# VectorE's sum of the third output bank in tiles 2 to 4 put behind the third token chunk's normalisation, and batch 6's key turn behind the third product

## The chip, the cores and the metric

One NeuronCore of a Trainium2 chip runs the whole kernel; the other cores are idle. The metric is the device time of one execution in microseconds, as the median of several runs. The engines are TensorE (PE, matrix products; PEld is its weight load), VectorE (DVE), ScalarE (ACT), GpSimd (POOL) and SyncE (SP, which issues DMAs). Each has its own queue of instructions and works through it in order; semaphores hold an instruction until what it needs is there.

## The reference

Attention over keys and values that are pooled by eight, and behind it a feed-forward layer whose hidden units are the largest of three products:

```python
k_p = k.reshape(B, H, Sp, 8, D).mean(axis=3)      # B, H, S, D = 8, 8, 576, 64; Sp = 72
v_p = v.reshape(B, H, Sp, 8, D).mean(axis=3)
scores = q @ k_p.transpose(0, 1, 3, 2) / sqrt(D)
attn = softmax(scores)
x = (attn @ v_p).transpose(0, 2, 1, 3).reshape(B * S, H * D)     # 4608 tokens x 512
h = maximum(maximum(x @ w1, x @ w2), x @ w3)                     # 768 hidden units
out = h @ w_out                                                  # 4608 x 512
```

## The kernel before

**Two streams on one PE queue.** The attention goes batch by batch (eight of 576 tokens), the feed-forward layer by tiles of 512 tokens (nine, numbered 0 to 8). While PE works on tile n, the attention of batch n+1 is put between its products by hand. The kernel schedules nothing by itself: each engine's queue has its instructions in the order in which the Python code records them. For tiles 1 to 4 this order stands in the strings of `MIDDLE` (line 886), which `middle` (line 909) reads step by step; tile 5's first half is `block(5, LEAD, ...)` (line 939), and the rest follows another string, `ORDER`.

**The steps of a string.** `h` is the next product of the hidden layer (line 364, in tiles `pw`, ScalarE's relu on line 370, VectorE's maximum on line 372). `s0` to `s7` are the scores of one head (line 220, then exp on ScalarE). `v0` to `v4` are the five token chunks of a batch: `values` multiplies weights by values into a PSUM tile `pav` (line 270), VectorE takes the reciprocal `rcp` of the sums (line 276) and multiplies it in, which gives `xn` (line 278; this is the chunk's normalisation). `x0` to `x4` turn `xn` into `xT` with a transposing DMA on SP's queue (line 255). `T` turns a batch's queries with such a DMA (line 304). `k` is the key turn: `keys` transposes the pooled keys `kp` on PE into the PSUM tile `pkt` (line 201), and `turn_k` copies it into the two key tensors `kz` (line 210), first two copies on VectorE, then two on ScalarE; the second pair waits for the first. Tokens such as `k7<` and `v6+2` load and fold inputs on GpSimd's queue.

**The output of tiles 2 to 4 by seven products.** With w1 folded into w_out, a tile's output is one product over 1280 columns (`xT` and `hT`), and it is taken as a 2 by 2 block product with seven products in place of eight. `outs(i, 0, 1)` in `middle` issues product `i` for both 128-token rows `m` (ten matmuls, line 718); product 2 comes as two halves, `2l` and `2h` (five matmuls each). Products 1, 6, 5 and 3 add up in one PSUM bank `oA`, 7 and 4 in `oC`, and 2 has `oB`. What becomes of a product stands in `evict` (line 722):

```python
if i in (1, 5, 6, 3):
    copy(int(i in (5, 3)), lo if i in (1, 3) else hi)     # ScalarE, line 728
elif i == 2:
    plus(0, lo, "B")                                      # VectorE, line 731
elif i == 4:
    plus(0, hi, "C")
if i in (5, 7) and (12 - i, m) in done:
    plus(1, hi, "C")
```

So after product 5 ScalarE copies `oA` into the result tile `osb`, and VectorE adds the third bank `oC` to it as soon as that copy is done. In the string of tiles 2 and 3, chunk `v3` follows product 5, then come `2h`, `v4`, 3 and 4. In tile 4 chunks `v3` and `v4` follow product 5, then come `2h`, batch 6's key turn `6:k`, 3 and 4.

**What is shared.** PSUM tiles come from small rings: `att` (two tiles) serves the scores, the `pav` of each chunk and `pkt`; `pw` (three tiles) serves the hidden products and the banks `oB` and `oC`; `tr` (one tile) serves `oA`. A tile is written again only when its last reader is done. So `pkt` in tile 4 waits for `xn` of chunk `v3`, product 4 waits for the reader of `oC`, and the second and third hidden products of the next tile wait for the readers of `oB` and `oC`. Right after tile 4, block 5 issues one hidden product, then the first scores of batch 6 (which read both `kz` tensors), then the second hidden product.

Of the kernel before, what the change touches and what calls it, by code (L numbers as in the profile page):

```python
# [14 lines left out]
def kernel(  # L15
# [46 lines left out]
    def psum(shape, dtype, name, tag, bufs):  # L62
        return pools[-1].tile(shape, dtype, name=name, tag=tag, bufs=bufs)
# [86 lines left out]
    def tokens(t0, t1, k0=0, k1=KCH):  # L150

        t0, t1 = t0 % RING, (t1 - 1) % RING + 1
        assert t0 < t1
        return xT[:, k0:k1, t0:t1]
# [244 lines left out]
    def new_two():  # L399
        return sb3.tile([128, 2, C], F32, name="osb", tag="osb", bufs=3)  # L400
# [127 lines left out]
    PA, BC, PO = ("pa", 2), ("bc", 1), ("po", 1)  # L528
# [32 lines left out]
    def turns(n):  # L561
        return (pad3 if n % 2 else pad)[:, 0:4]
# [17 lines left out]
    def out_w(z, r0, r1):  # L580

        i, j = divmod(z, 2)
        c = slice(HALF * i, HALF * i + HALF)
        return (wm_sb[:, 2 * j + r0:2 * j + r1, c] if r1 <= 2
                else wo_sb[:, JH * j + r0 - 2:JH * j + r1 - 2, c])

    def out_s(z):
        return so_new[0][:, z - 1]
# [56 lines left out]
    def out_seven(n):  # L645

        mid = len(pools) < 3
        if mid:
            o = {}
        else:  # L650
            o = sb2.tile([128, 2304], F32, name="ob", tag="et")[:, 0:2048].rearrange(
                "p (j m c) -> p j m c", j=2, m=2)
            o = [o[:, 0], o[:, 1]]
        lo, hi = slice(0, HALF), slice(HALF, C)
        banks, done = {}, set()

        def store(e, j, c):
            for u in range(2):
                b, g = divmod(2 * (4 * n + 2 * j) + u, NG)
                pair = g + 2 < NG and GS[g + 2] == GS[g] + 4  # L660
                for m in range(0, 2, 1 + pair):
                    b, g = divmod(2 * (4 * n + 2 * j + m) + u, NG)
                    dst = out[S * b:S * b + S, :].rearrange("(r g) c -> r g c", g=NG)
                    e.dma_start(out=dst[:, GS[g]:GS[g] + 4 * pair + 1:4, c],
                                in_=o[j][64 * u:64 * u + 64, m:m + 1 + pair, c])

        def bank(of, m):
            if n < LAST:
                if of not in banks:
                    if mid:  # L670
                        tag = TR if of == "A" else PW
                        banks[of] = psum([128, 2, HALF], F32, name=f"o{of}", tag=tag[0],
                                         bufs=tag[1])
                    elif of == "A":
                        banks["A"] = psum([128, 2, 2, HALF], F32, name="oA", tag="val",
                                          bufs=1)[:, 0]
                    else:
                        tag = (PO, SC)[of == "C"]
                        banks[of] = psum([128, 2, HALF], F32, name=f"o{of}", tag=tag[0],
                                         bufs=tag[1])  # L680
                return banks[of]
            if (of, m) not in banks:
                tag = {"A": PA, "B": SC, "C": BC if m == 0 else SC}[of]
                banks[of, m] = psum([128, 2, HALF], F32, name=f"o{of}", tag=tag[0],
                                    bufs=tag[1])[:, 0:1]
            return banks[of, m]

        def product(i, *ms):
            if mid:
                for r in range(5):  # L690
                    for m in ms:
                        matmuls(i, m, (r,))
            else:
                for m in ms:
                    matmuls(i, m)
            done.update((i, m) for m in ms)
            if not mid:
                evict(i, ms)
            elif (i, 1) in done:
                evict(i, (0, 1))  # L700

        def matmuls(i, m, rows=range(5)):
            of = "B" if i == 2 else "C" if i in (4, 7) else "A"
            p = bank(of, m)[:, m if n < LAST else 0]
            za, zb = PRODUCTS[i]
            for r in rows:
                c = slice(128 * m, 128 * m + 128)
                if isinstance(zb, str):
                    z = int(zb[1]) - 1
                    left = (tt_all[0][:, z, r, c] if mid else  # L710
                            turns(n)[:, z, r, c] if r < 2 else th[n][z][:, r - 2, c])
                else:
                    at = HALF * (zb % 2) + 128 * m
                    left = (tokens(NB * n + at, NB * n + at + 128)[:, 2 * (zb // 2) + r] if r < 2
                            else hTs[n][:, JH * (zb // 2) + r - 2, at:at + 128])
                right = (out_s(int(za[1]))[:, r] if isinstance(za, str)
                         else out_w(za, r, r + 1)[:, 0])
                nc.tensor.matmul(  # L718
                    p, left, right, stop=(r == 4), skip_group_check=True,
                    start=(i in FIRST and r == 0 and (m == 0 or n == LAST)))  # L720

        def evict(i, ms):
            m, at = ms[0], slice(ms[0], ms[-1] + 1)

            def copy(j, c):
                if j not in range(len(o)):
                    o[j] = new_two()
                nc.scalar.copy(out=o[j][:, at, c], in_=bank("A", m))  # L728

            def plus(j, c, of):  # L730
                nc.vector.tensor_tensor(out=o[j][:, at, c], in0=o[j][:, at, c],
                                        in1=bank(of, m), op=ALU.add)

            def ended(*parts):
                return all((z, k) in done for z in parts for k in range(2))

            if i in (1, 5, 6, 3):
                copy(int(i in (5, 3)), lo if i in (1, 3) else hi)
            elif i == 2:
                plus(0, lo, "B")  # L740
            elif i == 4:
                plus(0, hi, "C")
            if i in (5, 7) and (12 - i, m) in done:
                plus(1, hi, "C")
            if n == LAST and i in (5, 7) and ended(5, 7):
                store(nc.sync, 1, hi)
            if n == LAST and i == 3 and ended(3):
                store(nc.scalar, 1, lo)
            if n < LAST and i in (5, 7, 3) and ended(5, 7, 3):
                store(nc.sync, 1, slice(0, C))  # L750
            if n == LAST and i in (2, 4) and ended(i):
                store((nc.gpsimd, nc.sync)[i // 4], 0, (lo, hi)[i // 4])
            if n < LAST and i in (2, 4) and ended(2, 4):
                store(nc.sync, 0, slice(0, C))

        return product
# [102 lines left out]
    def weave():  # L859

        products, seen = {}, {}
        for name in ORDER.split():
# [29 lines left out]
        2: """  # L892
            h k k5< q5< v5< h a1 a3 a2 a4 S S ! v3+2 h h s0 h s1 h s2 h s3 h s4 b1 f f ! k4+1 h s5
            h s6 h s7 h b2 b3 b4 ! k4+2 v4+1
            1 v0 x0 2l v1 x1 6 7 v2 x2 5:T 5 v3 x3 2h v4 x4 3 4
        """,
        3: """
            h k k6< q6< v6< h a1 a3 a2 a4 f ! v4+2 h h s0 h s1 h s2 h s3 h s4 b1 f ! k5+1 h s5
            h s6 h s7 h b2 b3 b4 ! k5+2 v5+1
            1 v0 x0 2l v1 x1 6:T 6 7 v2 x2 5 v3 x3 2h v4 x4 3 4  # L900
        """,
        4: """
            h k k7< q7< v7< h a1 a3 a2 a4 f ! v5+2 h h s0 h s1 h s2 h s3 h s4 b1 f ! k6+1 h s5
            h s6 h s7 h b2 b3 b4 f ! k6+2 v6+1
            1 v0 x0 v1 x1 2l 7:T 6 7 v2 x2 5 v3 x3 v4 x4 2h 6:k 3 4 v6+2 k7+3 v7+3
        """}
    folds = iter([f for wi in range(1, 3) for f in [fold_w(wi)] * 4])

    def middle(n):

        pieces, outs, out_tiles = hidden(n), None, project(n)
        for name in MIDDLE[n].split():
            if name == "h":
                next(pieces)
            elif name == "F":
                next(out_tiles)
            elif name == "f":
                next(next(folds))
            elif name == "!":
                held[:] = gate  # L920
            elif name.isdigit():
                outs = outs or out_seven(n)
                outs(int(name), 0, 1)
            elif name in ("2l", "2h"):
                outs = outs or out_seven(n)
                outs(2, "lh".index(name[1]))
            elif name[0] in "ab":
                sums_of(n, name)
            elif name[2:3] in ("<", "+"):
                pool_step(n, name)  # L930
            else:
                b, _, step = name.rpartition(":")
                do(int(b or n + 1), step)
        assert next(pieces, None) is None

    tt_all.append(const.tile([128, 4, 5, HALF], F16, name="tt", tag="tt"))
    for n in range(1, 5):
        middle(n)
# [12 lines left out]
    outs = out_seven(LAST)  # L951
# [36 lines left out]
```

## Time and profile before

| what | value |
| --- | --- |
| runs | 226.40, 226.49, 227.48 us; median 226.49 us |
| profiled execution | 226.51 us, of which 224.8 us are the span of the profile |
| PE busy | 215.1 us (96% of the span) |
| DVE, ACT, POOL busy | 149.4, 122.0, 139.8 us |
| tile 2's output products | about 90 to 99 us from the span's start |
| tile 3's | about 111 to 120 us |
| tile 4's | about 133 to 143 us |

Times are counted from the start of the span. A row of the timeline has the start, the length, the engine, the line, the operation with its tensors (out, arrow, in), the shape and how many instructions stand in the row; in brackets stands the engine's idle time before it and what ended it. Rows of PE overlap, since the next matmul begins before the last has drained.

### The profile page before, as it was taken

The page shows a single profiled execution, that of the slowest core. Times are in us where ns is not written, and L with a number is a line of the kernel's source. Part 1 is how long each engine was busy: PE and PEld are TensorE (multiplying, and loading weights), DVE is VectorE, ACT ScalarE, POOL GpSimd, SP SyncE. Part 2 cuts the span into 40 slices and gives each one's busy share as a digit, 9 for nine tenths or more (in the row PEclk, how much of TensorE's full clock was granted, in tenths as well). Part 3 has the DMA queues.
Part 4 walks back from the last instruction along what each step waited for, and adds up shares of the span by engine and source line. Part 5 has one row for each costly group of instructions (what it writes and reads, how often), then busy time and mean ns, then how long its engine had stood idle before and what let it go on. Part 6 is the DMA issues. An engine that isn't in the chain of part 4 may idle for free.

```text
span 224.8 us, 4685 instructions
## 1 busy us (share of the span) xinstructions
PE 215.1 (96%) x1806; PEld 146.6 (65%) x1807; DVE 149.4 (66%) x292; ACT 122.0 (54%) x221; POOL 139.8 (62%) x111
## 2 busy tenths in 40 slices
PE   7788999999999999999999998899999999999993
PEld 2477745557655545875596567555677777788882
DVE  4668877037594395786579668636667886898840
ACT  2277524755875478238733862484786446554330
POOL 7974400999949967787768757999600903772020
PEclk9999999999999999999999999999999999999999
DMA  6999999989749999749999998963341533200266
GB/s 175 209 197 197 204 207 205 206 152 231 143 105 163 235 201 226 127 105 160 242 206 175 167 263 115 172 172 57 71 103 28 123 63 86 47 3 0 62 199 163
DMA packets 50710, 33.54 MB, mean 149 GB/s; under 512 B 27040, under 2 KB 46368, under 8 KB 50688
## 3 DMA queue, kind: packets, MB, share of 16 engines
q0 software_dynamic: 20304, 16.98, 48.1%
q1 hardware_dynamic: 29936, 15.87, 31.8%
q10 hardware_dynamic: 448, 0.39, 0.7%
q8 instruction: 14, 0.23, 0.4%
q14 instruction: 8, 0.07, 0.1%
HBM read 34.60 MB, written 9.44 MB: 196 GB/s over the span
## 4 chain that ended last, share of the span: by engine, by line
PE 71%; DMA 12%; POOL 11%; issue 2%; DVE 1%; ACT 1%; POOLq 0%
PE pw L364 21%; PE oA L718 10%; DMA vt<-in_v_dram 8%; PE pA L794 7%; PE po L418 7%; PE oC L718 5%; PE po L414 5%; PE psc L220 4%; DMA mw<-in_moe_w_dram 4%; PE pC L794 3%; PE pav L270 3%; POOL half L163 3%; PE oB L718 2%; POOL half L164 2%; PE pB L794 2%
## 5 line engine op out<-in xcount | busy, mean ns | idle before, releaser
L364 PE MATMUL pw<-xT,mw 128*128 128x512 f16 (+1 forms) x336 | 72.8, 349 | 0.3 <-ACT xT L264 0.2
L364 PEld LDWEIGHTS <-mw 128*128 128x128 f16 x336 | 31.6, 98 | 20.4 <-issue 0.6
L372 DVE TENSOR_TENSOR hT<-t,pw 128x512 f16<-128x512 f16 (+1 forms) x42 | 25.4, 608 | 23.8 <-ACT et L225 16.4
L225 ACT ACTIVATE et<-psc 72x576 f16<-72x576 f32 (+2 forms) x54 | 35.1, 660 | 6.4 <-PE psc L220 6.3
L163 POOL TENSOR_TENSOR half<-vt 72x2048 f32<-72x2048 f16 x7 | 28.4, 4061 | 13.8 <-DMA vt<-in_v_dram 13.3
L164 POOL TENSOR_TENSOR half<-half 72x1024 f32<-72x1024 f32 (+1 forms) x13 | 27.3, 2098 | 10.7 <-DVE rcp L276 6.1
L370 ACT ACTIVATE t<-pw 128x512 f16<-128x512 f32 (+1 forms) x42 | 22.5, 537 | 14.7 <-PE pw L364 14.3
L278 DVE TENSOR_TENSOR xn<-pav,rcp 128x512 f16<-128x512 f32 x40 | 27.6, 691 | 1.4
L220 PE MATMUL psc<-qT,kz 128*128 128x320 bf16 (+2 forms) x120 | 22.6, 278 | 1.1 <-DVE qT L196 0.9
L418 PE MATMUL po<-mwo,hT 128*128 128x512 f16 (+1 forms) x102 | 23.5, 367 | 0.0
L220 PEld LDWEIGHTS <-kz 128*128 128x128 bf16 x143 | 13.1, 98 | 13.6 <-ACT qT L196 1.1
L163 POOL TENSOR_TENSOR half<-ktFalse 96x1536 f32<-96x1536 f16 x6 | 18.8, 3131 | 4.0 <-issue 2.9
L800 ACT CAST pad<-pA 128x512 f16<-128x512 f32 x27 | 15.5, 587 | 7.2 <-PE pA L794 7.0
L566 POOL TENSOR_TENSOR pad<-xT 128x256 f16<-128x256 f16 x8 | 5.9, 734 | 21.7 <-ACT pad L800 12.9
L270 PEld LDWEIGHTS <-et 72*128 72x128 f16 x320 | 15.3, 98 | 3.6 <-issue 0.4
L276 DVE RECIPROCAL rcp<-pav 128x8 f32<-128x8 f32 x40 | 8.1, 202 | 14.1 <-PE pav L270 13.9
L270 PE MATMUL pav<-vp,et 72*128 72x65 f16 x320 | 16.6, 194 | 0.1
L414 PE MATMUL po<-wm,xT 128*128 128x512 f16 (+1 forms) x68 | 16.6, 366 | 0.0
L728 ACT COPY osb<-oA 128x512 f32<-128x512 f32 x12 | 7.0, 585 | 16.7 <-PE oA L718 16.7
L423 ACT COPY osb<-po 128x512 f32<-128x512 f32 (+1 forms) x16 | 9.2, 573 | 12.0 <-PE po L418 11.3
L774 DVE SCALAR_TENSOR_TENSOR hT<-pad 128x512 f16<-128x512 f16 x18 | 14.1, 797 | 2.3 <-ACT pad L804 1.9
L794 PEld LDWEIGHTS <-sw 128*128 128x128 f16 x144 | 13.6, 98 | 2.5
(122 smaller groups left out, 382.4 us busy)
## 6 DMA issues: line engine op xcount, KB each, us to landing
out_dram<-osb SPq DMA_DIRECT2D x38, 128.0 KB, 5.2
ktFalse<-in_k_dram POOLq DMA_DIRECT2D x7, 576.0 KB, 8.3
qb<-in_q_dram POOLq DMA_DIRECT2D x7, 576.0 KB, 12.0
vt<-in_v_dram POOLq DMA_DIRECT2D x7, 576.0 KB, 16.7
mw<-in_moe_w_dram POOLq DMA_DIRECT2D x9, 256.0 KB, 9.3
out_dram<-osb SPq DMA_DIRECT2D x8, 256.0 KB, 5.6
ktTrue<-in_k_dram SPq DMA_DIRECT2D x3, 384.0 KB, 5.1
out_dram<-ob SPq DMA_DIRECT2D x8, 128.0 KB, 2.5
```

The source lines that it names most:

```text
L163: yield e.tensor_tensor(out=f, in0=t[:, :, 0:4, :], in1=t[:, :, 4:8, :], op=ALU.add)
L164: yield e.tensor_tensor(out=f[:, :, 0:2, :], in0=f[:, :, 0:2, :], in1=f[:, :, 2:4, :], op=ALU.add)
L220: nc.tensor.matmul(out, kz_all[b % 2][f % 2][rows, h, :], qTs[b][rows, n + i0:n + i1, 64 * (h % 2):64 * (h % 2) + 64], start=True, stop=True)
L225: nc.scalar.activation(out=out, in_=in_, func=FT.Exp, scale=1.0 / 64.0)
L270: nc.tensor.matmul(pav[:, h // 4, 65 * (h % 4):65 * (h % 4) + 65], ets[b][:, h, c0:c0 + 128], vp_all[:, b, h, :], start=True, stop=True)
L278: nc.vector.tensor_tensor(out=xn, in0=pv[:, :, :, 0:D], in1=rcp.to_broadcast([128, 2, 4, D]), op=ALU.mult)
L364: mm = nc.tensor.matmul(pw, w_sb[wi][:, kc, bass.ts(jc, 128)], x[:, kc], start=(kc == 0), stop=(kc == KCH - 1))
L372: nc.vector.tensor_tensor(out=hT[:, jc, c0:c1], in0=t, in1=pw, op=ALU.max)
L414: nc.tensor.matmul(po, tokens(128 * m, 128 * m + 128)[:, kc], wm_sb[:, kc, c], start=(kc == 0), stop=False)
L418: nc.tensor.matmul(po, hT[:, jc, bass.ts(mm, 128)], wo_sb[:, jc, c], start=False, stop=(jc == JCH - 1))
L718: nc.tensor.matmul(p, left, right, stop=(r == 4), skip_group_check=True, start=(i in FIRST and r == 0 and (m == 0 or n == LAST)))
L794: mm = nc.tensor.matmul(p[:, w], a[:, kc, bass.ts(g, 128)], b[:, kc, :], start=(i in FIRST and w + kc == 0), stop=(w + kc == 2), skip_grou ...
```

## The change

In tiles 2 to 4 product 5's copy on ScalarE stays where it was. VectorE's sum of `oC` after it becomes a step of its own, `e5`, recorded behind chunk `v3`'s normalisation. VectorE's sum of `oB` becomes a step `e2`, recorded behind `v4`. In tiles 2 and 3 chunk `v4` also moves ahead of `2h`, and in tile 4 `2l` moves ahead of `v1`. In tile 4 the key turn `6:k` moves from ahead of product 3 to behind it, and `e2` comes behind the key turn. No instruction is added or dropped. The order on SP's and GpSimd's queues stays the same. On ScalarE's queue only the two key copies and the copy of product 3 change places in tile 4.

```diff
@@ product
+            if not ms:
+                evict(i, (0, 1), True)
+                return
             if mid:
...
             if not mid:
                 evict(i, ms)
-            elif (i, 1) in done:
+            elif i != 2:
                 evict(i, (0, 1))
@@ evict
-        def evict(i, ms):
+        def evict(i, ms, summed=False):
...
-            if i in (1, 5, 6, 3):
+            if summed:
+                plus(i == 5, (lo, hi)[i == 5], "BC"[i == 5])
+            elif i in (1, 5, 6, 3):
                 copy(int(i in (5, 3)), lo if i in (1, 3) else hi)
...
-            if i in (5, 7) and (12 - i, m) in done:
+            if not mid and i in (5, 7) and (12 - i, m) in done:
                 plus(1, hi, "C")
@@ MIDDLE, tile 2
-            1 v0 x0 2l v1 x1 6 7 v2 x2 5:T 5 v3 x3 2h v4 x4 3 4
+            1 v0 x0 2l v1 x1 6 7 v2 x2 5:T 5 v3 x3 e5 v4 x4 2h e2 3 4
@@ MIDDLE, tile 3
-            1 v0 x0 2l v1 x1 6:T 6 7 v2 x2 5 v3 x3 2h v4 x4 3 4
+            1 v0 x0 2l v1 x1 6:T 6 7 v2 x2 5 v3 x3 e5 v4 x4 2h e2 3 4
@@ MIDDLE, tile 4
-            1 v0 x0 v1 x1 2l 7:T 6 7 v2 x2 5 v3 x3 v4 x4 2h 6:k 3 4 v6+2 k7+3 v7+3
+            1 v0 x0 2l v1 x1 7:T 6 7 v2 x2 5 v3 x3 e5 v4 x4 2h 3 6:k e2 4 v6+2 k7+3 v7+3
@@ middle
+            elif name in ("e2", "e5"):
+                outs(int(name[1]))
```

## The prediction

> **What bounds the kernel now.** I read the page first: the span, the busy times and the engines' shares of the chain that ended last.
>
> ```profile
> span 224.8 us, 4685 instructions
> PE 215.1 (96%) x1806; PEld 146.6 (65%) x1807; DVE 149.4 (66%) x292; ACT 122.0 (54%) x221; POOL 139.8 (62%) x111
> PE 71%; DMA 12%; POOL 11%; issue 2%; DVE 1%; ACT 1%; POOLq 0%
> ```
>
> PE is busy for 96% of the span and carries most of the chain, so an edit of VectorE's order is worth only what it takes from PE's idle time. I therefore asked for PE's busy time in the three stretches that the edit touches (the output products of tiles 2, 3 and 4).
>
> ```profile
> 88.30:99.00 10.70, 10.70 (x120) 9.01 (x119) 7.60 (x17) 4.10 (x7) 9.05 (x4) 1.00 0.69 120
> 110.10:120.40 10.30, 10.30 (x118) 8.81 (x117) 7.15 (x17) 3.71 (x7) 7.92 (x4) 1.00 1.18 229
> 131.70:143.30 11.60, 10.34 (x121) 8.72 (x119) 8.93 (x19) 2.92 (x6) 8.95 (x5) 1.00 0.91 177
> ```
>
> After the stretch come its length and PE's busy time; the clock column reads 1.00. In tiles 2 and 3 PE is never idle: there is nothing to gain there, only something to lose. In tile 4 it is idle for 11.60 - 10.34 = 1.26 us. The waits from 138 to 145 us say why.
>
> ```profile
> PE pkt L201 <- DVE rcp L276: 1.3, 1, 1.3
> DVE osb L731 <- ACT osb L728: 0.8, 1, 0.8
> PEld L220 <- ACT kz L210: 0.5, 1, 0.5
> ```
>
> One wait of 1.3 us at the key turn, and a smaller one at the next scores, behind ScalarE's copies of the keys. The timeline has the whole story.
>
> ```profile
> 137.21 0.43 PE L270 MATMUL pav<-vp,et 72*128 72x65 f16 x8
> 137.68 0.21 DVE L276 RECIPROCAL rcp<-pav 128x8 f32<-128x8 f32 x1 [0.17 <-PE pav L270]
> 137.92 0.69 DVE L278 TENSOR_TENSOR xn<-pav,rcp 128x512 f16<-128x512 f32 x1
> ...
> 138.57 0.69 PE L270 MATMUL pav<-vp,et 72*128 72x65 f16 x16
> 138.77 0.58 ACT L728 COPY osb<-oA 128x512 f32<-128x512 f32 x1 [1.86 <-PE oA L718]
> ...
> 139.31 0.49 PE L718 MATMUL oB<-mwo,hT 128*128 128x256 f16 x3
> 139.38 0.69 DVE L731 TENSOR_TENSOR osb<-osb,oC 128x512 f32<-128x512 f32 x1 [0.78 <-ACT osb L728]
> 139.99 0.20 DVE L276 RECIPROCAL rcp<-pav 128x8 f32<-128x8 f32 x1
> 140.22 0.69 DVE L278 TENSOR_TENSOR xn<-pav,rcp 128x512 f16<-128x512 f32 x1
> ...
> 140.83 0.20 DVE L276 RECIPROCAL rcp<-pav 128x8 f32<-128x8 f32 x1
> ...
> 141.06 0.29 PE L201 MATMUL pkt<-ident,kp 96*128 96x96 bf16 x3 [1.26 <-DVE rcp L276]
> ...
> 141.19 0.60 PE L718 MATMUL oA<-so,xT 128*128 128x256 f16 x4
> ...
> 141.67 0.68 DVE L731 TENSOR_TENSOR osb<-osb,oB 128x512 f32<-128x512 f32 x1
> ...
> 142.27 0.97 DVE L210 COPY kz<-pkt 64x288 bf16<-64x288 bf16 x2
> 142.28 0.60 PE L718 MATMUL oC<-wm,tt 128*128 128x256 f16 x4
> ...
> 143.37 1.03 PE L364 MATMUL pw<-xT,mw 128*128 128x512 f16 x4
> 143.57 0.69 DVE L731 TENSOR_TENSOR osb<-osb,oC 128x512 f32<-128x512 f32 x1 [0.34 <-PE oC L718]
> 143.60 0.97 ACT L210 COPY kz<-pkt 64x288 bf16<-64x288 bf16 x2 [4.25 <-PE oC L718]
> ...
> 144.75 1.03 PE L364 MATMUL pw<-xT,mw 128*128 128x512 f16 x4
> ```
>
> The matmuls of chunks v3 and v4 start at 138.57. VectorE could normalise v3 at once, but ahead of that its queue holds the sum of the third bank, which waits until ScalarE's copy of product 5 ends (138.77 + 0.58 = 139.35). So v3's reciprocal comes at 139.99 and its xn ends at 140.22 + 0.69 = 140.91. The key turn needs the PSUM tile that this xn reads, and goes at 141.06; products 3 and 4, which need none of this, stand behind it on PE's queue.
>
> **The change, part by part.** Tile 4 first, worked out with the rows above.
>
> VectorE. From a chunk's first matmul to its reciprocal the row of v2 has 137.68 - 137.21 = 0.47, so v3's reciprocal goes at 138.57 + 0.47 = 139.04. From reciprocal to xn it is 0.24 (137.68 to 137.92), from xn or a sum to the next instruction 0.61 (140.22 to 140.83; 139.38 to 139.99). Hence v3's xn 139.28 to 139.97, the sum e5 from 139.89 to 140.58 (ScalarE's copy ended at 139.35, so it no longer waits), v4's reciprocal 140.50, its xn 140.74, the two key copies at 140.74 + 0.61 = 141.35 if pkt is there, ending at 141.35 + 0.97 = 142.32 in place of 143.24. Then the sums of the second and third bank, about 142.3 to 143.0 and 142.9 to 143.6. Two things bring the copies forward: 139.38 - 139.04 = 0.34 of waiting at the head, and 0.60 of the second bank's sum, which now stands behind them.
>
> PE. The half product 2h issues its last three matmuls from 139.31; at 1.09 / 10 = 0.109 each (ten of product 3 from 141.19 to 142.28) the next can go at 139.64. Product 3 takes its place there, until 140.73; it accumulates on oA, whose reader ended at 139.35. The key turn then finds its tile free (xn ended at 139.97) and takes 141.19 - 141.06 = 0.13; product 4 goes at 140.86, after e5's end at 140.58, and the next tile's first hidden product at 141.95 in place of 143.37: 1.42 earlier. That the key turn's cover is good is seen from pkt: done by 140.73 + 0.29 = 141.02, ahead of the copies at 141.35.
>
> What is late next: ScalarE's key copies, which the next scores need. They follow VectorE's.
>
> ```profile
> 121.61 0.97 DVE L210 COPY kz<-pkt 64x288 bf16<-64x288 bf16 x2
> ...
> 122.67 0.96 ACT L210 COPY kz<-pkt 64x288 bf16<-64x288 bf16 x2 [0.59 <-DVE kz L210]
> ```
>
> Here they start 122.67 - 122.58 = 0.09 after VectorE's end; in tile 4 it was 143.60 - 143.24 = 0.36, for which no row gives a reason. With 0.09 they run from 142.41 to 143.38. The second hidden product started 144.75 - 144.57 = 0.18 after their end, so it now starts at 143.56: 1.19 earlier. With 0.36 it would be 143.83, 0.92 earlier. I take 0.09, which is what an identical pair showed in tile 3. So of the 1.42 that PE wins, 0.23 are given back in a longer wait at the first scores. ScalarE's copy of product 3, now ahead of its key copies, ends by about 141.6 and delays nothing.
>
> The other waits of the next tile: the second hidden product needs the reader of oB (about 143.0, against 143.56), the third the reader of oC (about 143.6, against 143.56 + 1.1 = 144.7). Both are covered, by 0.5 and 1.1. The move of 2l ahead of v1 costs nothing: VectorE takes v1 behind v0 either way. GpSimd and SP keep their order.
>
> Does the rest follow? One resource keeps its own time, GpSimd's fold of batch 7.
>
> ```profile
> 151.90 1.00 POOL L166 TENSOR_TENSOR kp<-half 96x384 bf16<-96x384 f32 x1
> ...
> 156.48 0.29 PE L201 MATMUL pkt<-ident,kp 96*128 96x96 bf16 x3
> ```
>
> Its keys are ready at 152.90 and used at 156.48, or 155.3 then: 2.4 of slack. Everything else behind tile 4 hangs on PE, so I let the 1.19 reach the end.
>
> The first hidden product also needs chunk x1 of batch 5 in xT.
>
> ```profile
> L255 SPq DMA_TRANSPOSE xT<-xn x2: 1208/1848/2487, 136.7 to 138.0; - x2
> DMA to landing us min/median/max: 3.7/4.0/4.3
> ```
>
> These are x0 and x1, issued at 136.7 and 138.0; the second landed 3.7 or 4.3 later, between 141.7 and 142.3, so at 141.95 it may be just there or 0.35 short. At the later end the first product waits, but the scores behind it still wait for ScalarE until 143.38, so the price is nothing at either end. The Trainium skill (Perfetto Trace Analysis, section "DMA Instruction — HWDGE (DVE, Sync)") says that the bar of such an instruction covers the making of descriptors and not the movement of data: by the bar (138.0 + 2.49 = 140.5) there would be 1.4 us to spare. The trace agrees with the page: the landing row is 1.2 us or more behind the bar, and the sum by it stays the same only because ScalarE is later still.
>
> Tiles 2 and 3. PE's order changes only between chunk v4 and 2h. The one new risk is product 4, which now waits for e5 behind v3.
>
> ```profile
> 95.76 0.42 PE L270 MATMUL pav<-vp,et 72*128 72x65 f16 x8
> ...
> 97.92 0.60 PE L718 MATMUL oC<-wm,tt 128*128 128x256 f16 x4
> ```
>
> With the same steps, v3's reciprocal goes at 95.76 + 0.47 = 96.23, xn at 96.47, e5 from 97.08 to 97.77. Product 4 follows at 97.92, and PE reacted to xn in tile 4 after 141.06 - 140.91 = 0.15. So it just fits: 0 to 0.1 lost per tile, nothing gained since PE is never idle there; I take 0. The sums of oB and oC end about where they did.
>
> **Sum.** 226.51 (profiled execution; span 224.8 plus 1.7 around it) - 1.19 = 225.3 us. The median of the runs shown, 226.49, is the same within 0.02. That is 0.53% less. About 0.5%, or 1.13 us, is what a measurement of this kernel can tell from no change.
>
> **Rivals.**
> 1. *ScalarE's copies take back more.* If the 0.36 of tile 4 is their habit in this place, the gain is 0.92, and with 0.1 lost in each of tiles 2 and 3 it is 0.7: 225.6 to 225.8, within 0.5%. For it speaks that the 0.36 stood in this tile; against it the 0.09 of tile 3.
> 2. *A transfer or a fold takes the place of the wait.* If x1 lands over 0.5 us later than in this run, or GpSimd's fold slips by over 2.4, the gain shrinks by each further 0.1: about 226.0 to 226.5. The transposing DMA of x1 took 2487 ns where the other took 1208, so it does vary; but a later landing than 4.3 is seen in neither.
> 3. *Slower: product 4 becomes the place.* If v3's normalisation in tiles 2 and 3 isn't early, because something else than the third bank's sum holds it, then e5 and the reader of oC are late, and PE stalls in stretches where it never did. Were v3's reciprocal to go 0.95 later, at 97.18, e5 would end at 98.72 and product 4 start at 98.87: 0.95 in each of two tiles, 1.9, less 1.19: 227.2. It decides from 0.15 us of lateness on and turns the sign at 0.75 in each tile. Against it speaks that VectorE sat idle for 0.8 ahead of that sum in tile 4, so nothing else was held up.
>
> **How the numbers follow.** The forecast has 0.62, rivals 1 and 2 together 0.31 (0.22 and 0.09), rival 3 has 0.07. The forecast's cases reach from 225.1 (PE keeps all of the 1.42) to 225.4; rivals 1 and 2 go to 226.5. I give 224.9 to 226.5: 0.2 below the first for the spread of the runs, and up to rival 2's end; rival 3 stays outside. Faster by over 0.5% is the forecast, 0.62; within 0.5% are rivals 1 and 2, 0.31; slower 0.07.
>
> **What would show it.** Right: the wait of the key turn for rcp is gone; PE's idle time from product 1 of tile 4 to the next tile's first hidden product falls from 1.26 to below 0.2; v3's reciprocal in tile 4 goes about 0.5 after its matmuls and e5 right behind its xn; the scores' wait for ScalarE's key copies grows from 0.5 to about 0.7. Wrong: an idle PE ahead of product 4 in tile 2 or 3, a gap ahead of the first hidden product of the next tile put down to xT, or a second hidden product that starts later than 143.9.

## The result and the profile after

| | before | after |
| --- | --- | --- |
| median of 22 runs each | 226.49 us | 225.93 us (225.21 to 226.25) |
| ratio after / before | | 0.9976, 95% interval 0.9967 to 0.9985 |
| profiled execution; span | 226.51; 224.8 us | 225.68; 224.0 us |

The changed kernel is faster by 0.24%, which is 0.54 us with an interval of 0.34 to 0.75. The forecast was 1.19 us. By the bound of 0.5% this lies within no change, the case to which the prediction gave 0.31.

The page of after, in the same order as before's: span, busy times, engines' shares of the chain that ended last.

```profile
span 224.0 us, 4682 instructions
PE 214.2 (96%) x1806; PEld 146.6 (65%) x1807; DVE 149.4 (67%) x292; ACT 122.4 (55%) x221; POOL 140.1 (63%) x111
PE 86%; DVE 5%; DMA 3%; ACT 2%; issue 1%; SPq 0%; DVEq 0%; ACTq 0%
```

PE is still the bound. The three stretches of output products (stretch, its length, PE's busy time first):

```profile
88.30:99.00 10.70, 10.70 (x120) 9.01 (x119) 7.96 (x17) 3.92 (x7) 9.05 (x4) 1.00 0.68 117
110.10:120.40 10.30, 10.30 (x119) 8.81 (x117) 7.59 (x16) 3.52 (x7) 7.92 (x4) 1.00 1.20 241
131.70:143.30 11.60, 11.32 (x126) 9.26 (x124) 9.52 (x20) 4.56 (x9) 8.96 (x5) 1.00 0.95 193
```

Tiles 2 and 3 have no idle PE, as before. In tile 4's stretch 11.60 - 11.32 = 0.28 us are idle in place of 1.26, and those 0.28 now lie at the next tile's first scores. The timeline of tile 4 after the change shows each step:

```profile
138.37 0.68 PE L270 MATMUL pav<-vp,et 72*128 72x65 f16 x16
138.84 0.21 DVE L276 RECIPROCAL rcp<-pav 128x8 f32<-128x8 f32 x1 [0.42 <-PE pav L270]
139.08 0.69 DVE L278 TENSOR_TENSOR xn<-pav,rcp 128x512 f16<-128x512 f32 x1
139.69 0.68 DVE L734 TENSOR_TENSOR osb<-osb,oC 128x512 f32<-128x512 f32 x1
140.53 0.29 PE L201 MATMUL pkt<-ident,kp 96*128 96x96 bf16 x3
141.12 0.96 DVE L210 COPY kz<-pkt 64x288 bf16<-64x288 bf16 x2
141.76 1.03 PE L364 MATMUL pw<-xT,mw 128*128 128x512 f16 x4
142.18 0.96 ACT L210 COPY kz<-pkt 64x288 bf16<-64x288 bf16 x2 [0.86 <-DVE kz L210]
143.19 0.10 PEld L220 LDWEIGHTS <-kz 128*128 128x128 bf16 x1 [0.69 <-ACT kz L210]
143.31 1.03 PE L364 MATMUL pw<-xT,mw 128*128 128x512 f16 x4
```

Chunk v3's matmuls start at 138.37, where before had 138.57: the whole profile lies 0.20 earlier at this point. This offset is there already ahead of the first sum that was moved (tile 2's chunk v3 starts at 95.57 in place of 95.76), and it differs from one execution to the next (in the experiments, from 0.69 earlier to 0.41 later, also where the code up to there is the same). So I take it off each difference below and call what remains the lead. The second hidden product starts at 143.31 in place of 144.75, which is 1.44 - 0.20 = 1.24 of lead. Tile 4 therefore gave what was forecast, and the lead is lost later. The chain that ended last says where (start, length, what). After:

```profile
156.65 1.31 PE po L418 x6
157.97 0.59 ACT pad L805
159.65 1.39 DVE pad L566
161.07 0.60 PE pA L799 x4
161.67 1.29 PE po L418 x6
...
219.52 0.67 PE po L418 x6
```

and the same three groups of `po` before, with the product ahead of the second:

```profile
158.08 1.29 PE po L418 x6
...
162.03 0.44 PE pA L794 x4
162.47 1.29 PE po L418 x6
...
220.32 0.67 PE po L418 x6
```

At the first the lead is 158.08 - 156.65 - 0.20 = 1.23, at the second 162.47 - 161.67 - 0.20 = 0.60, and it is still 0.60 at the last. So 0.63 us are lost between 156.65 and 161.67. In after that stretch of the chain leaves PE for ScalarE and VectorE. PE's own waits from 130 us on are these two (us in total, times, longest us), and before has neither of them:

```profile
PE pA L799 <- DVE pad L566: 0.5, 1, 0.5
PE psc L220 <- ACT kz L210: 0.3, 1, 0.3
```

The second is the 0.28 of tile 4's stretch. The first lies in the stretch that loses the lead. Line 566 is VectorE's fold of x for tile 6's seven products (the `T` of `ORDER`): four 16-bit subtractions of two SBUF tensors each. The timeline of after at this place:

```profile
159.19 0.42 DVE L566 TENSOR_TENSOR pad<-xT 128x512 f16<-128x512 f16 x1
159.35 1.39 POOL L166 TENSOR_TENSOR vp<-half 72x512 f16<-72x512 f32 x1
159.65 1.37 DVE L566 TENSOR_TENSOR pad<-xT,pad 128x512 f16<-128x512 f16 x1
...
161.07 0.60 PE L799 MATMUL pA<-pad,sw 128*128 128x256 f16 x4 [0.47 <-DVE pad L566]
```

and before:

```profile
159.55 1.27 POOL L166 TENSOR_TENSOR vp<-half 72x512 f16<-72x512 f32 x1
160.63 0.48 DVE L566 TENSOR_TENSOR pad<-xT 128x512 f16<-128x512 f16 x1
161.14 0.42 DVE L566 TENSOR_TENSOR pad<-xT,pad 128x512 f16<-128x512 f16 x1
```

GpSimd's last step of folding batch 7's values (line 166) has kept its place: 159.35 against 159.55, the offset and no more. VectorE's fold hangs on PE and came 159.19 against 160.63, earlier by 1.44. Before, it began when GpSimd's step had 0.19 left to run. Now the two begin within 0.16 of each other, the second subtraction lasts 1.37 us in place of 0.42, and PE waits for it. PE is idle for 0.47, and the four matmuls behind the wait then take their full 0.60 on the chain in place of 0.44, since no matmuls ahead of them overlap with them: 0.47 + 0.16 = 0.63.

### The profile page after: what moved, and what is told of

It is laid out like the page before. It is cut to its first block, busy times and chain, and to the rows that moved or that the text cites. A ratio compares the mean times of both kernels' runs of the same rounds, so it can differ in the third digit from the quotient of the medians.

```text
span 224.0 us, 4682 instructions
## 1 busy us (share of the span) xinstructions
PE 214.2 (96%) x1806; PEld 146.6 (65%) x1807; DVE 149.4 (67%) x292; ACT 122.4 (55%) x221; POOL 140.1 (63%) x111
## 4 chain that ended last, share of the span: by engine, by line
PE 86%; DVE 5%; DMA 3%; ACT 2%; issue 1%; SPq 0%; DVEq 0%; ACTq 0%
PE pw L364 26%; PE po L418 9%; PE oA L721 9%; PE pA L799 7%; PE psc L220 6%; PE po L414 5%; PE oC L721 4%; PE pav L270 4%; PE pC L799 4%; DMA ktTrue<-in_k_dram 3%; PE pm L351 2%; PE oB L721 2%; PE pxt L261 2%; PE pB L799 2%; PE pqt L194 1%; DVE xn L278 1%
## 5 line engine op out<-in xcount | busy, mean ns | idle before, releaser
L776 DVE TENSOR_TENSOR pad<-pad,pC 128x512 f16<-128x512 f16 x18 | 12.3, 685 | 3.9 <-PE pC L799 3.6
```

## The experiments

Theory A says that the lead is lost there and by that: GpSimd's step holds up VectorE's subtraction. Against it stands that the lead was never whole, that it is lost elsewhere, or that the long subtraction only stands beside another wait. Each run was timed in five rounds beside the kernel before. Leads are taken from one profiled execution each, as above, the ratio from the timed runs. Gains in us are worked out from the ratios; before's median was 226.20 in the rounds of runs 1 to 4 and 226.47 in those of runs 5 to 8, and differences of medians come out up to 0.26 us away from them.

**1. Change kept, GpSimd held.** The last step of batch 7's value fold is recorded behind the fourth subtraction and waits for it.

```diff
@@ line 566
-            e.tensor_tensor(out=t[i], in0=a, in1=b, op=ALU.subtract)
+            gate[:] = [e.tensor_tensor(out=t[i], in0=a, in1=b, op=ALU.subtract)]
@@ ORDER
-        k7 1a F F 2a T 1b v62 ...
+        k7 1a F F 2a T p 1b v62 ...
@@ weave
+            elif name == "p":
+                held[:] = gate
+                pool_step(7, "v7+1")
@@ MIDDLE, tile 4
-            ... 3 6:k e2 4 v6+2 k7+3 v7+3
+            ... 3 6:k e2 4 v6+2 k7+3 v7+2
```

> The changed kernel, with the last of GpSimd's three steps of batch 7's value fold (the sum that writes vp) held until VectorE's four subtractions of tile 6's x (line 566) are done. Theory A (these two ran at the same time in the changed kernel and VectorE's second subtraction took 1.37 us in place of 0.42, which cost 0.6 of the 1.24 us won in tile 4): all four subtractions take 0.4 to 0.5 us, PE no longer waits for them, and the time falls by a further 0.5 to 0.6, to about 1.1 to 1.2 us below the kernel before (ratio 0.995). Theory B (the subtraction is slow for a reason of its own, such as the transposes that write xT): it stays at about 1.4 us and the time stays at about 0.55 below. Theory C (the missing 0.6 is spread over tiles 2 and 3 or is only a difference between single executions): the subtraction becomes quick but the time stays at about 0.55 below.

Measured: 224.95 us, ratio 0.9937 (0.9919 to 0.9956), which is 1.43 us below before (1.0 to 1.8; 1.25 by the medians). The interval lies clear of that of the change without the hold, 0.9967 to 0.9985. The timeline:

```profile
137.88 0.69 PE L270 MATMUL pav<-vp,et 72*128 72x65 f16 x16
...
159.15 0.42 DVE L566 TENSOR_TENSOR pad<-xT,pad 128x512 f16<-128x512 f16 x1
...
160.39 1.26 POOL L166 TENSOR_TENSOR vp<-half 72x512 f16<-72x512 f32 x1 [1.64 <-DVE rcp L276]
```

The subtraction is back at 0.42, GpSimd starts behind the fold, and no wait of PE for line 566 is left. The last `po` of its chain:

```profile
218.40 0.67 PE po L418 x6
```

The offset is 138.57 - 137.88 = 0.69, and 220.32 - 218.40 - 0.69 = 1.23 of lead reach the end, all of tile 4's 1.24. The hold itself costs nothing that shows.

**2. The same hold without the change.**

```diff
@@ as in 1, on the kernel before; MIDDLE, tile 4
-            ... 2h 6:k 3 4 v6+2 k7+3 v7+3
+            ... 2h 6:k 3 4 v6+2 k7+3 v7+2
```

> The kernel before, with the same hold of GpSimd's last fold step. In the kernel before the two met only for 0.2 us (first subtraction 0.48 in place of 0.42, none of it waited for). Theory A: no change, 0 to 0.1 us faster. A rival, by which holding the fold helps any kernel of this build (another cause than the shift of tile 4), expects 0.5 us or more here too.

Measured: 226.51 us, ratio 1.0005 (0.999 to 1.0021). The hold is worth nothing by itself. What the first run has below before is therefore the change's own gain, and the hold only keeps it.

**3. The change in tile 4 alone.**

```diff
@@ MIDDLE, tiles 2 and 3
-            ... 5 v3 x3 e5 v4 x4 2h e2 3 4
+            ... 5 e5 v3 x3 2h e2 v4 x4 3 4
```

> Only tile 4 has the new order; in tiles 2 and 3 the sums of the third and second bank stand where they stood before. Theory A: the same as the whole change, about 0.55 us below the kernel before. Theory C (the moves in tiles 2 and 3 cost what is missing): 1.0 to 1.2 us below.

Measured: 225.87 us, ratio 0.9987 (0.9974 to 1.0001). The interval holds the expected 0.55 us and, just, no gain at all; the profile is clearer, with 1.23 of lead at the second hidden product and 0.60 at the end. The group of line 566 shows the same collision (shortest, middle and longest in ns):

```profile
L566 DVE TENSOR_TENSOR pad<-xT,pad x2: 412/893/1374, 159.7 to 161.4; 128x512 f16<-128x512 f16 x2
```

**4. The change in tiles 2 and 3 alone.**

```diff
@@ MIDDLE, tile 4
-            1 v0 x0 2l v1 x1 7:T 6 7 v2 x2 5 v3 x3 e5 v4 x4 2h 3 6:k e2 4 ...
+            1 v0 x0 v1 x1 2l 7:T 6 7 v2 x2 5 e5 v3 x3 v4 x4 2h e2 6:k 3 4 ...
```

> Only tiles 2 and 3 have the new order; tile 4 is as before. Theory A: 0, at most 0.1 us either way, and product 4 follows product 3 on PE without a gap. Theory C: 0.4 to 0.6 us slower.

Measured: 226.51 us, ratio 1.0008 (0.9996 to 1.0019): no gain, and no loss that is clear of the noise (0.1 us faster to 0.4 slower). Its last `po` starts at 220.36 with an offset of 0.05 later, a lead of 0.01. Tile 4's stretch has its 1.26 of idle PE again:

```profile
131.70:143.30 11.60, 10.34 (x120) 8.68 (x118) 8.93 (x19) 2.98 (x6) 8.94 (x5) 1.00 1.04 207
```

**5 and 6. The two halves of tile 4's change.** Run 5 moves the sum behind v3's normalisation and leaves the key turn ahead of product 3. Run 6 moves the key turn and leaves the sums where they were. Tiles 2 and 3 stay as changed in both.

```diff
@@ MIDDLE, tile 4, run 5
-            ... 5 v3 x3 e5 v4 x4 2h 3 6:k e2 4 ...
+            ... 5 v3 x3 e5 v4 x4 2h e2 6:k 3 4 ...
@@ MIDDLE, tile 4, run 6
-            1 v0 x0 2l v1 x1 7:T 6 7 v2 x2 5 v3 x3 e5 v4 x4 2h 3 6:k e2 4 ...
+            1 v0 x0 v1 x1 2l 7:T 6 7 v2 x2 5 e5 v3 x3 v4 x4 2h e2 3 6:k 4 ...
```

> The whole change but for the key turn: in tile 4 it stands ahead of product 3 again, and the second bank's sum ahead of it; only the third bank's sum is behind chunk v3. By the rows of the kernel before, VectorE's key copies then end at 142.9, ScalarE's at 144.0, and the next tile's second hidden product starts 0.6 us earlier than in the kernel before (the whole change: 1.24). Theory A adds a stop: GpSimd's last fold step ends at the same time in every version, and VectorE's fold of x gets through only then, so whatever tile 4 wins beyond about 0.6 is lost. So this half of the change gives the same end as the whole: 0.5 to 0.6 us below the kernel before. A theory by which a fixed share of each gain is lost expects 0.25 to 0.3.

> The other half in tile 4: the key turn stands behind product 3, but the sums of the third and second bank go where they went before (ahead of v3's normalisation and ahead of the key copies). VectorE's queue is as long as before ahead of the key copies, so these end at the same time; only the 0.27 us goes that ScalarE's copies started late in the kernel before (0.36 behind VectorE's end in place of 0.09). Expected: the next tile's second hidden product 0 to 0.3 us earlier, the time 0 to 0.3 us below the kernel before, although PE's wait at the key turn is no longer 1.26.

| | ratio (95%) | lead at the second hidden product | lead at the end |
| --- | --- | --- | --- |
| the sum alone (5) | 0.9977 (0.9964 to 0.9991) | 0.37 | 0.28 |
| the key turn alone (6) | 0.9981 (0.9968 to 0.9994) | 0.29 | 0.27 |
| both, tile 4 only (3) | 0.9987 (0.9974 to 1.0001) | 1.23 | 0.60 |

The intervals of the three ratios overlap, so what follows rests on the leads. Both halves together make 0.66, the whole change in tile 4 makes 1.23. The key copies show where the rest is (times with the offset taken back, so that they compare with before's). VectorE's begin at 142.27 in before, 141.92 in run 5, 142.27 in run 6 and 141.32 in after. In run 5 they come 0.35 earlier, and the sum of the second bank still stands ahead of them, which is the 0.60 between it and after. In run 6 they come no earlier; its 0.29 is in the main ScalarE's start, 0.09 behind VectorE's end in place of 0.36. After has all three: 0.35 + 0.60 + 0.27 = 1.22. No run moved the second bank's sum alone, so the 0.60 is a difference between two runs. Run 5 has less lead than the 0.6 that I expected, as ScalarE's copies still start late:

```profile
141.89 0.96 DVE L210 COPY kz<-pkt 64x288 bf16<-64x288 bf16 x2
143.22 0.96 ACT L210 COPY kz<-pkt 64x288 bf16<-64x288 bf16 x2 [3.89 <-DVE kz L210]
...
159.50 1.28 POOL L166 TENSOR_TENSOR vp<-half 72x512 f16<-72x512 f32 x1
159.63 0.69 DVE L776 TENSOR_TENSOR pad<-pad,pB 128x512 f16<-128x512 f16 x1 [1.69 <-ACT pad L805]
160.23 0.82 DVE L566 TENSOR_TENSOR pad<-xT 128x512 f16<-128x512 f16 x1
```

They start 143.22 - 142.85 = 0.37 behind VectorE's end, where the whole change has 0.10. Both runs end with a smaller collision: here the first subtraction lasts 0.82, in run 6 0.75, which took 0.09 and 0.02 of the lead. So it is not a fixed share of each gain that is lost (0.63 of 1.24 in after, 0.09 of 0.37 here). The time of run 5, 0.52 below before with an interval of 0.2 to 0.8, holds both values that its expectation set against each other.

**7. The collision made longer.** The last two steps of the value fold, instead of one, are held until VectorE's sum just ahead of the subtractions, so that they run beside them.

```diff
@@ line 776
-            nc.vector.tensor_tensor(out=out, in0=kept(i, g), in1=p, op=ALU.add)
+            gate[:] = [nc.vector.tensor_tensor(out=out, in0=kept(i, g), in1=p, op=ALU.add)]
@@ ORDER
-        k7 1a F F 2a T 1b v62 ...
+        k7 1a F F 2a p T 1b v62 ...
@@ weave
+            elif name == "p":
+                held[:] = gate
+                pool_step(7, "v7+2")
@@ MIDDLE, tile 4
-            ... 3 6:k e2 4 v6+2 k7+3 v7+3
+            ... 3 6:k e2 4 v6+2 k7+3 v7+1
```

> The changed kernel with the meeting made longer: GpSimd's second and third step of batch 7's value fold (2.36 and 1.27 us) are held until VectorE's sum just ahead of its fold of x, so that both run beside the four subtractions. Theory A: the second subtraction lasts until the second fold step ends (about 2.4 us in place of 1.37), or until the third ends (about 3.7), PE waits 1.0 to 2.3 us longer for it, and the time is 1.0 to 2.3 us above the changed kernel, that is 0.4 to 1.8 above the kernel before. Without contention between the two engines: no change against the changed kernel, about 0.55 below the kernel before, since these values are not used before 168 us.

Measured: 227.27 us, ratio 1.0047 (1.003 to 1.0063), 1.06 us slower than before, within the 0.4 to 1.8 that theory A expected. PE waits 1.6 for line 566:

```profile
159.62 0.42 DVE L566 TENSOR_TENSOR pad<-xT 128x512 f16<-128x512 f16 x1
159.85 2.39 POOL L164 TENSOR_TENSOR half<-half 72x1024 f32<-72x1024 f32 x1 [3.00 <-DVE pad L776]
160.07 2.45 DVE L566 TENSOR_TENSOR pad<-xT,pad 128x512 f16<-128x512 f16 x1
162.32 1.33 POOL L166 TENSOR_TENSOR vp<-half 72x512 f16<-72x512 f32 x1
162.45 1.49 DVE L566 TENSOR_TENSOR pad<-xT 128x512 f16<-128x512 f16 x1
```

A longer GpSimd step makes a longer subtraction, 2.45 beside 2.39, and the next step catches the next one. PE also waits 0.5 for a chunk's normalisation, and by the chain this is the same collision's, since VectorE's queue holds that chunk behind the subtractions:

```profile
160.07 4.20 DVE pad L566 x3
...
165.17 0.42 PE pav L270 x8
```

A third wait is not the collision's. PE waits 0.7 at the next tile's first hidden product for a transposed chunk: x0 and x1 landed 4.6 to 5.5 us after their issue in this execution, 3.7 to 4.3 in before and in after. The edit does not touch that place. The lead was 0.83 behind it in place of 1.24, and the profiled execution, 227.82, is the longest of its runs.

**8. The hold of run 1, and the first scores one product later.** In after PE still waits for ScalarE's key copies at the next tile's first scores. Here batch 6's first scores go behind the second hidden product.

```diff
@@ LEAD, beside the edits of 1
-    LEAD = {0: [(6, "s0")], 1: [(6, "s1")], 2: [(6, "s2")], 3: [(6, "s3")],
+    LEAD = {1: [(6, "s0 s1")], 2: [(6, "s2")], 3: [(6, "s3")],
```

> The changed kernel with the hold of GpSimd's last fold step, and with batch 6's first scores moved one hidden product later (the first two heads together behind the second hidden product of block 5), so that PE no longer waits 0.28 us for ScalarE's key copies there. If that wait is all that is left of the 1.42 us that PE won: 0.2 to 0.3 us faster than with the hold alone, which is 1.4 to 1.6 below the kernel before. If ScalarE's two exps in a row delay the hidden products behind them instead: the same as with the hold alone (1.1 to 1.3 below) or slower.

Measured: 224.56 us, ratio 0.9927 (0.9913 to 0.9942), the lowest time of all versions. In its timeline the two hidden products are one row, without a gap, and no wait for ScalarE's copies is left:

```profile
141.65 2.07 PE L364 MATMUL pw<-xT,mw 128*128 128x512 f16 x8
```

Its last `po` starts at 218.51 by the chain. 220.32 - 218.51 less the offset of 0.38 (its chunk v3 starts at 138.19) is a lead of 1.43 at the end, against 1.23 in run 1. The profiles thus put 0.2 on the later scores. The timed ratios, 0.9937 and 0.9927, have intervals that overlap, so this last step is not shown by time alone.

## Why the prediction was right in tile 4 and wrong at the end

**Tile 4's sum: right.** VectorE's chain ran as worked out. Forecast less the offset of 0.20, against measured: v3's reciprocal 138.84 and 138.84, xn 139.08 and 139.08, the sum 139.69 and 139.69, the key copies 141.15 and 141.12, the first hidden product 141.75 and 141.76, the second 143.36 and 143.31. The lead was 1.24 where 1.19 was forecast.

**What is late next: right.** The first scores wait for ScalarE's key copies, 0.7 on PE's weight load, as forecast. The copies start 0.10 behind VectorE's, not 0.36, so rival 1 did not come about in the changed kernel; in run 5, with the key turn at its old place, it did.

**Tiles 2 and 3: right.** PE has no idle time there, and run 4 puts their part at nothing within its interval. Rival 3 (product 4 late) did not occur: in tile 2 the sum e5 ended 0.17 ahead of product 4.

**The step that failed** is under "Does the rest follow?": "Everything else behind tile 4 hangs on PE, so I let the 1.19 reach the end." I had looked for what GpSimd delivers late, found its keys with 2.4 us of slack, and stopped there. The fold that mattered was the next on its queue, the values of batch 7. They were not late. They were in the way: work that hangs on PE moved 1.24 us forward into a step that keeps its own time, VectorE's second subtraction took 1.37 in place of 0.42, and 0.63 of the lead went there; 0.60 reached the end. The trace of before had the sign: VectorE's first subtraction at 160.63 lasted 0.48 where the next took 0.42, with GpSimd's step ending at 160.82, so any lead moved it further into that step. Runs 1 and 2 show this cause by taking it away (the whole 1.23 comes through, and the hold alone is worth nothing), and run 7 by enlarging it (2.45, and PE's wait 1.6 in place of 0.5).

**The rivals and chances.** The time came out where rivals 1 and 2 lay, by neither of their mechanisms. Rival 2 named a GpSimd fold, but as one that slips by over 2.4; it did not slip. Its other half, a late x1, shows in no wait of after, but run 7's execution had it: 0.7 of waiting, at a landing later than the 4.3 that the prediction took as the latest seen. The bound of 0.5% for what can be told from no change was too wide: the interval of the ratio is 0.1% either way. No rival had two engines that meet without either waiting for the other's result, and such a case should have taken a good part of the 0.62.

**How far it could have been known beforehand.** The trace of before has the same meeting, with its price, at 62 us. There VectorE's fold of the output weights (line 599) meets the value fold of another batch; its first operation takes 1.34 us, the next, of the same size, 0.42:

```profile
62.10 1.27 POOL L166 TENSOR_TENSOR vp<-half 72x512 f16<-72x512 f32 x1
62.31 1.34 DVE L599 TENSOR_TENSOR so<-wm 128x512 f16<-128x512 f16 x1
63.68 0.42 DVE L599 TENSOR_TENSOR so<-so,wm 128x512 f16<-128x512 f16 x1
```

The long one ended 63.65 - 63.37 = 0.28 behind GpSimd's step. With the fold of x pulled forward by 1.19, its first subtraction would begin at 159.44, ahead of GpSimd's step at 159.55, and the second inside it. It would end at about 160.82 + 0.28 = 161.10. PE's product that reads it takes 0.60, so the `po` behind it could not start before 161.70, and in before it started at 162.47: at most 0.77 of the 1.19 would be left. That is an estimate from rows of before alone; 0.60 was measured.

## What to carry to other kernels

When an edit pulls a stage forward, look not only for what it will now wait for, but for what it will now run beside: lay the moved rows over those engines that keep their own time, and look for VectorE and GpSimd at SBUF together. Where they meet, hold the one with slack behind the other with a wait; here that cost nothing that shows and more than doubled the gain. The kernel before has such waits elsewhere: `!` in the strings of `MIDDLE` makes GpSimd's next fold step wait for the fold operation that was recorded last for VectorE. `ORDER`, to which the fold of x belongs, has none.

## What the runs showed of the hardware

**VectorE beside GpSimd.** In every case seen, a 16-bit sum or difference of two SBUF tensors of 128x512 that began with 0.19 us or more of a GpSimd tensor step left ended 0.27 to 0.29 us behind that step's end, however long it had still to run. Some of the cases:

| | GpSimd's step ends | VectorE's begins, lasts | ends behind it |
| --- | --- | --- | --- |
| before | 63.37 | 62.31, 1.34 | 0.28 |
| before | 160.82 | 160.63, 0.48 | 0.29 |
| after | 160.74 | 159.65, 1.37 | 0.28 |
| run 5 | 160.78 | 160.23, 0.82 | 0.27 |
| run 7 | 162.24 | 160.07, 2.45 | 0.28 |
| run 7 | 163.65 | 162.45, 1.49 | 0.29 |
| run 8 | 159.05 | 158.82, 0.52 | 0.29 |

One that began ahead of GpSimd's step took its 0.42 (159.62 in run 7), and so did one that began with under 0.1 left of a step (159.19 in after, with 0.08 left of the step ahead; 158.70 in run 1, with 0.05). A VectorE sum that reads one of its inputs from PSUM was not held: line 776 in run 5 began at 159.63, inside GpSimd's 159.50 to 160.78, and took the 0.69 that it takes in all runs. The Trainium skill (SBUF — State Buffer, section "SBUF: two separate sides") says that VectorE's operations with two SBUF inputs and GpSimd's share a pair of ports as an exclusive lock: the one that starts first has it for the whole instruction, the other is blocked. The rows of the table agree. The other direction shows less: GpSimd's step that began at 159.35, with VectorE's subtraction still running until 159.61, lasted 1.39 in place of 1.26 to 1.28, which is 0.11 to 0.13 longer for 0.26 of overlap. A full block would have cost 0.26, which this row does not show.

**ScalarE's late start.** ScalarE's key copies began 0.36 to 0.37 behind VectorE's where ScalarE had been idle for 3.9 us or more (tile 4 in before, run 5), and 0.08 to 0.10 where it had been idle for 2.0 us or less (tile 3 in before, after, run 6, and batch 7's key turn in before):

```profile
142.66 0.96 ACT L210 COPY kz<-pkt 64x288 bf16<-64x288 bf16 x2 [1.81 <-PE pw L364]
```

This is run 6, behind VectorE's copies that ended at 142.57. In the changed kernel the copy of product 3 now runs on ScalarE shortly ahead of the key copies, and this 0.27 went with it. That the idle time is the cause is only argued: no run changed it alone. In before the profile puts ScalarE's wait down to product 4 (`<-PE oC`), which ended at 143.54, just ahead of the copies; in run 5 product 4 ended at 142.56 and VectorE's copies at 142.85, and ScalarE's began as late behind these, so product 4 is not the cause there.
